# Score bounds in four column tiles and three rounds of 256 columns, and block 1's input added by VectorE in the tail

## The chip, the cores and the metric

The kernel runs on one core of a Trainium2 chip. A core has five engines with a queue each: TensorE (PE; its weight loads are listed as PEld), VectorE (DVE), ScalarE (ACT), GpSimd (POOL) and SyncE (SP), which here only issues DMAs. The metric is the time of one execution on the device in microseconds; smaller is better. Beside several timed executions there is one profiled execution, from which every duration in this document comes.

## The reference

The input `x` has 2048 rows of 640 values. It is normalized by row, goes through an attention with 32 heads of 20 values in four segments of 512 rows (softmax inside a segment, a linear memory over the segments before), and is multiplied by the gate of a gated feed-forward network:

```python
    x = A_x
    xn = _layernorm(x, axis=-1)
    s = _A_ref(xn, A_wq, A_wk, A_wv, A_wo, A_beta)
    g = _silu(_B_ref(xn, B_w_gate, B_w_up, B_w_down))
    return x + s * g
```

In `_A_ref`, for each segment:

```python
        logits = jnp.einsum('bhqd,bhkd->bhqk', qs, ks) * scale + mask
        p = _softmax(logits, axis=-1)
        a_dot = jnp.einsum('bhqk,bhkd->bhqd', p, vs)
        pq = phi(qs)
        num = jnp.einsum('bhld,bhde->bhle', pq, M)
        den = jnp.einsum('bhld,bhd->bhl', pq, z)[..., None] + 1e-06
        a_mem = num / den
        o = g * a_mem + (1.0 - g) * a_dot
```

## The kernel before

**Stages.** A segment is 512 rows (`L`), in four blocks `j` of 128. For each segment the kernel normalizes `x`, projects Q, K (`psq`) and V (`psv`), computes scores and exponentials, the products with V (`ApsT`), the memory part (`am`, `dm`), the gate and up products (`gp`, `up`, then `hT`), the down product (`yp`, then `aa`), and the output projection (`sp`). The product of `aa` and `sp` is added to `x` (the tile `xt`) and stored.

**Slots.** The scores are cut into units of four row tiles. A unit fills the PSUM tile `Sps` (one buffer of four banks), ScalarE takes its exponential into `pt`, GpSimd masks the diagonal. There are 81 units, and the loop over `slot` puts one of them after another on TensorE; in between, the rest of the work is issued by hand-set due times (`TIMES`) and by a rate. All instructions keep the order in which the program issues them on their engine. In a slot before a `visits` entry, `ORDER["columns"]` makes `mm` issue each matmul as four of 32 output columns, one for each column tile of the array (128*32 in the profile).

**Score bounds.** The exponential is taken without a row maximum; instead an upper bound of each score is subtracted inside the matmul. `q_abs` (L320) takes the absolute values of Q into `aq`, in two pieces of Q's five 128-row slices: slices 0 to 2 first, 3 and 4 later. `do_K` keeps the largest absolute value of each K row (`kabs`), and `bound` (L326) spreads them into a stationary operand `ik` of 32 columns, with a minus sign. `bound_mm` (L335) multiplies slice `c` of `ik` and `aq` into rows `32*(c%3)` and on of `cps`: three partial sums, in column tiles 0, 1 and 2, with 512 columns for each matmul. ScalarE casts `cps` to `cb` (L338), a DMA writes it to DRAM (`Bd`, L339), and `bound_dma` (L344, four DMAs for each half of the eight head groups) brings the partial rows behind the 20 rows of each head in `QT`. `KT` holds ones there, so `scores` (L546), with 23 rows, adds the three partial sums. The SP queue carries these DMAs between those of `relayout` (L313) for Q and K.

**PSUM.** Apart from `Sps`, all products take turns in four buffers (`ps_d`, tag `d`); a product waits until the buffer's last user has been read.

**Tail.** The last segment's `sp` are issued by hand at the end of the program. `tail_piece` (L532) multiplies half a block (128x320), VectorE multiplies it into `aa` (L535), then an engine adds `xt` (L538), and a queue stores (L541). Before the change GpSimd adds blocks 0 and 1 whole, when the second half is done, and block 2 in halves; VectorE adds block 3 in halves. Blocks 0, 1 and 3 are stored by SP, block 2 by ScalarE's queue. `tail_T4` transposes a piece for two blocks, with a copy by ScalarE (L524).

In the sections that follow, 1a and 1b are the halves of block 1, and so on; a "product" is L535, an "addition" L538.

Of the kernel before, what the change touches and what calls it, by code (L numbers as in the profile page):

```python
# [9 lines left out]
P = 128  # L10
D = 640
H = 32
DH = 20
E1 = DH + 1
NSEG = 4
L = 512
F = 1536
DC = D // P
# [63 lines left out]
def kernel(  # L82
# [14 lines left out]
    nc = tc.nc  # L97
    x2 = A_x.flatten_outer_dims()
    o2 = out.flatten_outer_dims()
# [11 lines left out]
    dpool = ctx.enter_context(tc.tile_pool(name="dscratch", bufs=1, space=bass.MemoryType.DRAM))  # L111
    Qd = [dpool.tile([D, L], BF, name=f"Qd{i}") for i in range(2)]
    Kd = [dpool.tile([D, L], BF, name=f"Kd{i}") for i in range(2)]
    Xd = [dpool.tile([L, D], BF, name=f"Xd{i}") for i in range(2)]
    Bd = [dpool.tile([3 * H, L], BF, name=f"Bd{i}") for i in range(2)]
    OTd = [dpool.tile([D, L], BF, name=f"OTd{i}") for i in range(2)]
    Od = [dpool.tile([L, D], BF, name=f"Od{i}") for i in range(2)]

# [5 lines left out]
    xt_of, xnT_of = {}, {}  # L124
# [24 lines left out]
    Wo = cpool.tile([P, DC, D], BF, name="Wo")  # L149
# [34 lines left out]
    KT = cpool.tile([P, NG, L], BF, name="KT")  # L184
    QT = cpool.tile([P, NG, L], BF, name="QT")
# [91 lines left out]
    seg = {}  # L277
# [51 lines left out]

    def bound_mm(n):  # L330
        ik, aq = seg[n]["bound"]
        cps = ps_d.tile([3 * H, L], F32, name="cps", tag="d")
        for c in range(DC):
            i = c % 3
            nc.tensor.matmul(cps[H * i:H * i + H, :], lhsT=ik[:, c, :], rhs=aq[:, c, :],  # L335
                             start=(c < 3), stop=(c >= 2), tile_position=(0, H * i), skip_group_check=True)
        cb = stg.tile([3 * H, L], BF, name="cb")
        nc.scalar.copy(cb[:], cps[:])  # L338
        nc.sync.dma_start(Bd[n % 2][:], cb[:])  # L339

    def bound_dma(n, half):
        src = Bd[n % 2][:].rearrange("(i r g) n -> r i g n", i=3, r=4)
        for r in range(4):
            nc.sync.dma_start(QT[32 * r + DH:32 * r + DH + 3, 4 * half:4 * half + 4, :],  # L344
                              src[r][:, 4 * half:4 * half + 4, :])

    def do_V(n, j, half, evac):
# [111 lines left out]
    def finish(steps):  # L459
        for _ in steps:  # L460
            pass
# [51 lines left out]
    def tail_T():  # L513
        nc.sync.dma_start_transpose(out=seg[NSEG - 1]["oTm"][:, 3, :], in_=Od[(NSEG - 1) % 2][:, C3:C4])

    def tail_add():
        oTm = seg[NSEG - 1]["oTm"][0:CUT, 3, :]
        nc.vector.tensor_tensor(oTm, oTm, seg[NSEG - 1]["oT"][0:CUT, 3, :], op=ALU.add)

# [3 lines left out]
            nc.tensor.transpose(po[:, j - j0, :], seg[NSEG - 1]["odot"][:, j, C4:D], ident[:])  # L523
        nc.scalar.copy(seg[NSEG - 1]["oT"][:, DC - 1, j0 * P:j1 * P].rearrange("p (j t) -> p j t", t=P), po[:])  # L524

    def tail_piece(j, h0, h1, add, store=None, queue=None):

        s, hs = seg[NSEG - 1], slice(h0, h1)
        sp = ps_d.tile([P, HD], F32, name="sp", tag="d")
        for c in range(DC):  # L530
            oT = s["oTm" if c == 3 else "oT"]
            nc.tensor.matmul(sp[:, 0:h1 - h0], lhsT=oT[:, c, j * P:(j + 1) * P], rhs=Wo[:, c, hs],  # L532
                             start=(c == 0), stop=(c == DC - 1), skip_group_check=True)
        aa, xr = s["aa"][j], xt_of[NSEG - 1][:, j, :]
        nc.vector.tensor_tensor(aa[:, hs], aa[:, hs], sp[:, 0:h1 - h0], op=ALU.mult)  # L535
        if add is not None:
            a0 = store[0] if store else h0
            add.tensor_tensor(xr[:, a0:h1], aa[:, a0:h1], xr[:, a0:h1], op=ALU.add)  # L538
        if store:
            t0 = (4 * (NSEG - 1) + j) * P  # L540
            queue.dma_start(o2[t0:t0 + P, store[0]:store[1]], xr[:, store[0]:store[1]])  # L541

    def scores(unit):
        for r in range(4):
            for (g, kb, c0, ncol, q0) in unit:
                nc.tensor.matmul(Sps[:, r, c0:c0 + ncol],  # L546
                                 lhsT=KT[32 * r:32 * r + DH + 3, g, kb * P:(kb + 1) * P],
                                 rhs=QT[32 * r:32 * r + DH + 3, g, q0:L],
                                 start=True, stop=True, tile_position=(32 * r, 0))

    def exps(unit):
# [208 lines left out]
    SLOTS, SEG = len(units), 20  # L760
# [27 lines left out]
    def old_attend(slot):  # L788
        attend(NSEG - 1, units[slot][1], pts[slot])
# [17 lines left out]
    for n in range(NSEG):  # L807
        t0 = n * SEG

        def on(name, ns, fn, *items):  # L810
            times = TIMES[name]
            for i, it in enumerate(items):
                at(t0 + (times[i] if isinstance(times, (list, tuple)) else times), ns, fn, *it)

        if n >= 1:
            on("dot6", 0, dot_spill, (n - 1, 4, 7))
            on("load6", 0, out_load, (n - 1, 0, C4))
            on("dot7", 0, dot_spill, (n - 1, 7, 8))
            on("load7", 0, out_load, (n - 1, C4, D))
            if n >= 2:  # L820
                on("add", 0, out_add, (n - 1, 0, DC - 1), (n - 1, DC - 1, DC))
            on("out", V_NS, out_item, *[(n - 1, i) for i in range(8)])
            on("update", 700, m_update, (n - 1,))
            on("mem", MEM_NS, mem_part, *[(n, i % 4, i // 4) for i in range(8)])
            on("mem_spill", 0, mem_spill, (n,))
            on("mem_T_last" if n == NSEG - 1 else "mem_T", 0, mem_T, (n,))
            if n < NSEG - 1:
                on("k_tok", 0, k_tok, (n,))
        on("dot3", 0, dot_spill, (n, 0, 4))
        if n == NSEG - 1:  # L830
# [12 lines left out]
        on("V", V_NS, do_V, *[(m, i // 2, i % 2, EVAC[TIMES["V_eng"][i]]) for i in range(8)])  # L843
        on("k_spill0", 0, spill, (m, 0, nc.sync, None))
        on("k_lay0", 0, relayout, (m, 0, Kd, KT, nc.sync))
        on("q_spill0", 0, spill, (m, 0, None, nc.sync))
        on("q_lay0", 0, relayout, (m, 0, Qd, QT, nc.sync))
        on("q_spill1", 0, spill, (m, 1, None, nc.sync))
        on("k_spill1", 0, spill, (m, 1, nc.sync, None))
        on("q_abs", 0, q_abs, (m, 0, 3), (m, 3, DC))  # L850
        on("bound", 0, bound, (m,))
        on("bound_mm", C_NS, bound_mm, (m,))
        on("bound_lay0", 0, bound_dma, (m, 0))
        at(t0 + SEG - 0.003, 0, relayout, m, 1, Kd, KT, nc.sync)
        at(t0 + SEG - 0.002, 0, relayout, m, 1, Qd, QT, nc.sync)
        at(t0 + SEG - 0.001, 0, bound_dma, m, 1)
        for name, sg, key in (("phi_k", n, "ktok"), ("phi_q", m, "qt")):
            for i, (c0, c1) in enumerate(((0, 2), (2, 4 if key == "ktok" else 5))):
                for fn, t, a in zip((phi_min, phi_exp, phi_end), TIMES[name][i], ((sg, key, c0, c1), (), ())):
                    at(t0 + t, 0, fn, *a)  # L860
        if n + 2 < NSEG:
            on("load_x", 0, load_x, (n + 2,))
    at(SLOTS - 2.001, 0, tail_spill)
    at(SLOTS - 1.001, 0, tail_T)
    at(SLOTS - 0.001, 0, tail_add)

    events.sort(key=lambda e: e[:2])
    events = deque(events)
# [32 lines left out]
    for slot, (n, unit) in enumerate(units):  # L901
        if slot in visits:
            m, g, us = visits[slot]
# [24 lines left out]
    finish(held[1][3])  # L928
    tail_T4(0, 2)
    old_attend(SLOTS - 1)  # L930
    tail_piece(0, 0, HD, None)
    tail_piece(0, HD, D, nc.gpsimd, (0, D), nc.sync)
    finish(held[0][3])
    tail_piece(1, 0, HD, None)
    tail_piece(1, HD, D, nc.gpsimd, (0, D), nc.sync)
    tail_T4(2, 4)
    tail_piece(2, 0, HD, nc.gpsimd, (0, HD), nc.scalar)
    tail_piece(2, HD, D, nc.gpsimd, (HD, D), nc.scalar)
    tail_piece(3, 0, HD, nc.vector, (0, HD), nc.sync)
    tail_piece(3, HD, D, nc.vector, (HD, D), nc.sync)  # L940

_INS = ['A_x', 'A_wq', 'A_wk', 'A_wv', 'A_wo', 'A_beta', 'B_x', 'B_w_gate', 'B_w_up', 'B_w_down']
_OUTS = [((1, 2048, 640), 'bfloat16')]
# [24 lines left out]
```

## Time and profile before

| | |
|---|---|
| median of three runs | 320.7 us (320.14, 320.99, 320.7) |
| the profiled execution's own time | 319.95 us |
| its span, first to last instruction | 318.2 us |
| granted TensorE clock, mean | 0.997 |
| PE, DVE, ACT, POOL busy | 312.3, 229.3, 227.2, 136.6 us |
| `cps` matmuls | 20, of 379 to 390 ns |
| `cb` casts | 4, of 581 to 612 ns |
| additions on POOL in the tail | 2 of 128x640 (1392 ns), 2 of 128x320 (789 ns) |
| additions on DVE in the tail | 2 of 128x320 (597 ns in the mean) |

How to read it: the span is the time between the first and the last instruction of the profiled execution; its own time has what lies around that too. A matmul's duration has the passage through the array in it, and matmuls overlap; how fast they follow each other is read from their starts. In a timeline each line has the start and the duration in us, the engine, the line of the code, the operation, out<-in, the shape and a count; in square brackets stands the engine's idle time before it and what ended it. A line with a count over 1 covers several instructions in a row. The chain of waits goes back from the last instruction: at each step to what released it, or to the instruction before it on its engine.

### The profile page before, as it was taken

How to read it: one execution, taken by the hardware profiler on the slowest of the kernel's cores; microseconds unless marked ns; L12 is line 12 of the kernel's file. 1: busy time of each engine (PE TensorE's matmuls, PEld its weight loads, DVE VectorE, ACT ScalarE, POOL GpSimd, SP SyncE). 2: the span in 40 equal slices, each digit the busy share in tenths (PEclk: the TensorE clock that was granted, in tenths of full speed). 3: DMA queues.
4: the chain of work that ended last, by engine and by line, in shares of the span. 5: the costliest groups of instructions: out<-in, count | busy, mean ns of one | idle time of the engine just before them, and what ended most of it. 6: DMA issues, size and time to landing. Idle time of an engine off the chain costs nothing.

```text
span 318.2 us, 10079 instructions
## 1 busy us (share of the span) xinstructions
PE 312.3 (98%) x4244; PEld 167.1 (53%) x4244; DVE 229.3 (72%) x503; ACT 227.2 (71%) x229; POOL 136.6 (43%) x231
## 2 busy tenths in 40 slices
PE   8999999999999999999999999999999999999994
PEld 3544445665555445654675455545466545445673
DVE  6474356756869888997679999977787687634555
ACT  3723477787898877777998768678897766776730
POOL 1870036435263445334453454445433353535324
PEclk9999999999999999999999999999999999999998
DMA  8984986410752362406583373235723000350302
GB/s 256 355 333 140 305 217 178 108 41 2 217 150 71 105 149 91 123 23 194 182 206 101 115 128 111 79 129 190 179 86 115 19 23 31 119 126 2 100 19 82
DMA packets 56086, 41.36 MB, mean 130 GB/s; under 512 B 26953, under 2 KB 54665, under 8 KB 56041
## 3 DMA queue, kind: packets, MB, share of 16 engines
q1 hardware_dynamic: 53496, 35.97, 39.9%
q10 hardware_dynamic: 2544, 4.75, 4.1%
q8 instruction: 33, 0.54, 0.7%
q14 instruction: 13, 0.10, 0.1%
HBM read 19.90 MB, written 14.78 MB: 109 GB/s over the span
## 4 chain that ended last, share of the span: by engine, by line
PE 97%; ACT 1%; DVE 1%; issue 0%; ACTq 0%
PE up L130 11%; PE yp L130 11%; PE gp L130 10%; PE psq L130 10%; PE Sps L546 9%; PE gp L134 6%; PE up L134 6%; PE yp L134 6%; PE psv L130 6%; PE ApsT L570 5%; PE psq L134 4%; PE sp L130 3%; PE sp L134 3%; PE sp L532 2%; PE psv L134 1%; PE wps L642 1%
## 5 line engine op out<-in xcount | busy, mean ns | idle before, releaser
L554 ACT ACTIVATE pt<-Sps 128x2048 bf16<-128x2048 f32 (+1 forms) x81 | 150.3, 1856 | 40.8 <-PE Sps L546 36.0
L556 POOL TENSOR_SCALAR_AFFINE_SELECT pt<-pt 128x512 bf16<-128x512 bf16 x128 | 83.0, 664 | 158.0 <-ACT pt L554 157.9
L438 DVE SCALAR_TENSOR_TENSOR hT<-tg,up 128x512 bf16<-128x512 bf16 x48 | 32.4, 674 | 23.3 <-PE up L130 8.7
L130 PE MATMUL up<-xnT,Wu 128*128 128x512 bf16 x160 | 43.0, 380 | 0.0
L130 PE MATMUL yp<-Wd,hT 128*128 128x320 bf16 x257 | 40.1, 300 | 0.0
L130 PE MATMUL gp<-xnT,Wg 128*128 128x512 bf16 x150 | 39.3, 380 | 0.0
L427 ACT ACTIVATE tg<-gp 128x512 bf16<-128x512 f32 x48 | 28.6, 596 | 14.3 <-PE gp L130 11.0
L546 PE MATMUL Sps<-QT,KT 23*128 23x128 bf16 (+3 forms) x512 | 32.6, 301 | 0.2
L589 DVE STREAM_TRANSPOSE obT<-ob 128x512 bf16<-128x512 bf16 x30 | 21.1, 704 | 13.3 <-POOL ob L585 13.3
L130 PEld LDWEIGHTS <-hT 128*128 128x128 bf16 x257 | 23.5, 98 | 11.6 <-issue 3.0
L455 DVE SCALAR_TENSOR_TENSOR aa<-t,yp 128x320 bf16<-128x320 bf16 x32 | 15.3, 478 | 14.5 <-ACT t L454 14.3
L134 PE MATMUL gp<-xnT,Wg 128*32 128x512 bf16 x360 | 24.1, 380 | 0.0
L591 DVE STREAM_TRANSPOSE tb<-ApsT 128x512 f32<-128x512 f32 x30 | 21.2, 708 | 2.4 <-PE ApsT L570 2.1
L130 PEld LDWEIGHTS <-Wu 128*128 128x128 bf16 x160 | 14.3, 98 | 16.2 <-issue 3.2
L546 PEld LDWEIGHTS <-KT 23*128 23x128 bf16 x512 | 10.0, 92 | 24.5 <-issue 24.4
L570 PE MATMUL ApsT<-pt,V 128*32 128x512 bf16 (+2 forms) x480 | 22.7, 299 | 0.0
L130 PEld LDWEIGHTS <-Wg 128*128 128x128 bf16 x150 | 14.1, 98 | 16.0 <-issue 1.9
L134 PE MATMUL up<-xnT,Wu 128*32 128x512 bf16 x320 | 21.7, 380 | 0.0
L454 ACT ACTIVATE t<-yp 128x320 bf16<-128x320 f32 x32 | 13.9, 435 | 10.4 <-PE yp L130 8.7
L130 PE MATMUL psv<-Wv,xnT 128*128 128x320 bf16 x130 | 20.8, 299 | 0.3
L585 POOL TENSOR_TENSOR ob<-tb,rb 128x320 bf16<-128x320 f32 x27 | 19.8, 732 | 2.2
L134 PE MATMUL yp<-Wd,hT 128*32 128x320 bf16 x508 | 20.0, 300 | 0.0
(122 smaller groups left out, 449.9 us busy)
## 6 DMA issues: line engine op xcount, KB each, us to landing
KT<-Kd SPq DMA_DIRECT2D x32, 80.0 KB
QT<-Qd SPq DMA_DIRECT2D x32, 80.0 KB
out_dram<-xt SPq DMA_DIRECT2D x14, 160.0 KB
Wg<-in_B_w_gate_dram ACTq DMA_DIRECT2D x1, 1920.0 KB
Wu<-in_B_w_up_dram ACTq DMA_DIRECT2D x1, 1920.0 KB
xt<-in_A_x_dram SPq DMA_DIRECT2D x3, 640.0 KB
Wd<-in_B_w_down_dram SPq DMA_DIRECT2D x1, 1920.0 KB
Xd<-xn SPq DMA_DIRECT2D x12, 160.0 KB
```

The lines of the kernel that those rows point to most:

```text
L130: nc.tensor.matmul(out_, lhsT=lhsT, rhs=rhs, start=start, stop=stop, skip_group_check=True)
L134: nc.tensor.matmul(out_[cols], lhsT=lhsT[:, cols], rhs=rhs, start=start, stop=stop, tile_position=(0, 32 * r), skip_group_check=True)
L427: nc.scalar.activation(tg[:], gp[:], ACT.Tanh, scale=0.5)
L438: nc.vector.scalar_tensor_tensor(out=h[:], in0=seg[n]["tg"][:], scalar=1.0, in1=up[:], op0=ALU.add, op1=ALU.mult)
L455: nc.vector.scalar_tensor_tensor(out=s["aa"][j][:, hs], in0=t2[:], scalar=1.0, in1=yp[:], op0=ALU.add, op1=ALU.mult)
L546: nc.tensor.matmul(Sps[:, r, c0:c0 + ncol], lhsT=KT[32 * r:32 * r + DH + 3, g, kb * P:(kb + 1) * P], rhs=QT[32 * r:32 * r + DH + 3, g, q0: ...
L554: nc.scalar.activation(pt[:, :, 0:ntot], Sps[:, :, 0:ntot], ACT.Exp, scale=SCALE)
L556: nc.gpsimd.affine_select(out=pt[:, :, c0:c0 + P], in_=pt[:, :, c0:c0 + P], compare_op=ALU.is_ge, fill=0.0, base=0, pattern=[[0, 4], [1, P ...
L570: nc.tensor.matmul(ps[32 * r:32 * r + 32, q0:L], lhsT=Vflat[n % 2][:, off:off + 32], rhs=t[:, r, c0:c0 + ncol], start=(i == 0), stop=(i == ...
L585: nc.gpsimd.tensor_tensor(ob[:, :, 0:DH], tb[:, :, 0:DH], rb[:].unsqueeze(2).to_broadcast([P, L // 32, DH]), op=ALU.mult)
L589: nc.vector.transpose(s["obT", g // 4][:, g % 4, :], ob[:].rearrange("p b e -> p (b e)"))
L591: s["turn", g] = (lambda: nc.vector.transpose(tb[:].rearrange("p b e -> p (b e)"), ps[:]), quotients, turn_back)
```

## The change

`bound_mm` now makes four partial sums in four column tiles. Ten matmuls of 256 columns take the place of five of 512: slices 0 to 3 in column tiles 0 to 3, first for the left half of the columns, then for the right half; then slice 4 for the left half in column tile 0 and for the right half in column tile 1. `Bd`, `cb` and the rows in `QT` grow from three partial rows to four, and `scores` multiplies 24 rows. In segments 1 to 3 `q_abs` takes slices 0 to 3 first and slice 4 later; in segment 0 its pieces stay.

In the tail, block 1's `x` is added by VectorE in two halves, and no longer by GpSimd whole: 1a is added after product 1b, and 1b after product 2a. SP stores block 1 after that, whole as before. The additions of the other blocks stay with their engines.

```diff
-    Bd = [dpool.tile([3 * H, L], BF, name=f"Bd{i}") for i in range(2)]
+    Bd = [dpool.tile([4 * H, L], BF, name=f"Bd{i}") for i in range(2)]
...
     def bound_mm(n):
         ik, aq = seg[n]["bound"]
-        cps = ps_d.tile([3 * H, L], F32, name="cps", tag="d")
-        for c in range(DC):
-            i = c % 3
-            nc.tensor.matmul(cps[H * i:H * i + H, :], lhsT=ik[:, c, :], rhs=aq[:, c, :],
-                             start=(c < 3), stop=(c >= 2), tile_position=(0, H * i), skip_group_check=True)
-        cb = stg.tile([3 * H, L], BF, name="cb")
+
+        cps = ps_d.tile([4 * H, L], F32, name="cps", tag="d")
+        jobs = [(i, i, h) for h in range(2) for i in range(4)] + [(4, h, h) for h in range(2)]
+        for c, i, h in jobs:
+            hs = slice(h * L // 2, (h + 1) * L // 2)
+            nc.tensor.matmul(cps[H * i:H * i + H, hs], lhsT=ik[:, c, :], rhs=aq[:, c, hs],
+                             start=(c < 4), stop=(c == 4 or i != h), tile_position=(0, H * i),
+                             skip_group_check=True)
+        cb = stg.tile([4 * H, L], BF, name="cb")
         nc.scalar.copy(cb[:], cps[:])
         nc.sync.dma_start(Bd[n % 2][:], cb[:])
 
     def bound_dma(n, half):
-        src = Bd[n % 2][:].rearrange("(i r g) n -> r i g n", i=3, r=4)
+        src = Bd[n % 2][:].rearrange("(i r g) n -> r i g n", i=4, r=4)
         for r in range(4):
-            nc.sync.dma_start(QT[32 * r + DH:32 * r + DH + 3, 4 * half:4 * half + 4, :],
+            nc.sync.dma_start(QT[32 * r + DH:32 * r + DH + 4, 4 * half:4 * half + 4, :],
                               src[r][:, 4 * half:4 * half + 4, :])
...
-    def tail_piece(j, h0, h1, add, store=None, queue=None):
+    def tail_piece(j, half):
...
-        aa, xr = s["aa"][j], xt_of[NSEG - 1][:, j, :]
-        nc.vector.tensor_tensor(aa[:, hs], aa[:, hs], sp[:, 0:h1 - h0], op=ALU.mult)
-        if add is not None:
-            a0 = store[0] if store else h0
-            add.tensor_tensor(xr[:, a0:h1], aa[:, a0:h1], xr[:, a0:h1], op=ALU.add)
-        if store:
+        nc.vector.tensor_tensor(s["aa"][j][:, hs], s["aa"][j][:, hs], sp[:], op=ALU.mult)
+
+    def tail_add(j, h0, h1, eng, queue=None):
+
+        hs = slice(h0 * HD, h1 * HD)
+        xr = xt_of[NSEG - 1][:, j, hs]
+        eng.tensor_tensor(xr, seg[NSEG - 1]["aa"][j][:, hs], xr, op=ALU.add)
+        if queue is not None:
             t0 = (4 * (NSEG - 1) + j) * P
-            queue.dma_start(o2[t0:t0 + P, store[0]:store[1]], xr[:, store[0]:store[1]])
+            queue.dma_start(o2[t0:t0 + P, hs], xr)
 
     def scores(unit):
...
-                                 lhsT=KT[32 * r:32 * r + DH + 3, g, kb * P:(kb + 1) * P],
-                                 rhs=QT[32 * r:32 * r + DH + 3, g, q0:L],
+                                 lhsT=KT[32 * r:32 * r + DH + 4, g, kb * P:(kb + 1) * P],
+                                 rhs=QT[32 * r:32 * r + DH + 4, g, q0:L],
...
-        on("q_abs", 0, q_abs, (m, 0, 3), (m, 3, DC))
+        on("q_abs", 0, q_abs, (m, 0, 4), (m, 4, DC))
...
-    tail_piece(0, 0, HD, None)
-    tail_piece(0, HD, D, nc.gpsimd, (0, D), nc.sync)
+    tail_piece(0, 0)
+    tail_piece(0, 1)
+    tail_add(0, 0, 2, nc.gpsimd, nc.sync)
     finish(held[0][3])
-    tail_piece(1, 0, HD, None)
-    tail_piece(1, HD, D, nc.gpsimd, (0, D), nc.sync)
+    tail_piece(1, 0)
+    tail_piece(1, 1)
+    tail_add(1, 0, 1, nc.vector)
     tail_T4(2, 4)
-    tail_piece(2, 0, HD, nc.gpsimd, (0, HD), nc.scalar)
-    tail_piece(2, HD, D, nc.gpsimd, (HD, D), nc.scalar)
-    tail_piece(3, 0, HD, nc.vector, (0, HD), nc.sync)
-    tail_piece(3, HD, D, nc.vector, (HD, D), nc.sync)
+    tail_piece(2, 0)
+    tail_add(2, 0, 1, nc.gpsimd, nc.scalar)
+    tail_add(1, 1, 2, nc.vector)
+    t0 = (4 * (NSEG - 1) + 1) * P
+    nc.sync.dma_start(o2[t0:t0 + P, :], xt_of[NSEG - 1][:, 1, :])
+    tail_piece(2, 1)
+    tail_add(2, 1, 2, nc.gpsimd, nc.scalar)
+    tail_piece(3, 0)
+    tail_add(3, 0, 1, nc.vector, nc.sync)
+    tail_piece(3, 1)
+    tail_add(3, 1, 2, nc.vector, nc.sync)
```

The order of the instructions on every engine is otherwise the same as before; the old `tail_add`, which adds `oT` into `oTm` (L518), is now called `tail_sum`.

More of the change, by code (lines that the diff above doesn't have):

```diff
@@ L514, in tail_T, with tail_sum @@
         nc.sync.dma_start_transpose(out=seg[NSEG - 1]["oTm"][:, 3, :], in_=Od[(NSEG - 1) % 2][:, C3:C4])
-    def tail_add():
+    def tail_sum():
         oTm = seg[NSEG - 1]["oTm"][0:CUT, 3, :]
@@ L524, in tail_T4 @@
         nc.scalar.copy(seg[NSEG - 1]["oT"][:, DC - 1, j0 * P:j1 * P].rearrange("p (j t) -> p j t", t=P), po[:])
-    def tail_piece(j, h0, h1, add, store=None, queue=None):
-        s, hs = seg[NSEG - 1], slice(h0, h1)
+    def tail_piece(j, half):
+        s, hs = seg[NSEG - 1], slice(half * HD, (half + 1) * HD)
         sp = ps_d.tile([P, HD], F32, name="sp", tag="d")
@@ L531, in tail_piece @@
             oT = s["oTm" if c == 3 else "oT"]
-            nc.tensor.matmul(sp[:, 0:h1 - h0], lhsT=oT[:, c, j * P:(j + 1) * P], rhs=Wo[:, c, hs],
+            nc.tensor.matmul(sp[:], lhsT=oT[:, c, j * P:(j + 1) * P], rhs=Wo[:, c, hs],
                              start=(c == 0), stop=(c == DC - 1), skip_group_check=True)
-        aa, xr = s["aa"][j], xt_of[NSEG - 1][:, j, :]
-        nc.vector.tensor_tensor(aa[:, hs], aa[:, hs], sp[:, 0:h1 - h0], op=ALU.mult)
-        if add is not None:
-            a0 = store[0] if store else h0
-            add.tensor_tensor(xr[:, a0:h1], aa[:, a0:h1], xr[:, a0:h1], op=ALU.add)
-        if store:
+        nc.vector.tensor_tensor(s["aa"][j][:, hs], s["aa"][j][:, hs], sp[:], op=ALU.mult)
[4 more added lines that the diff above has]
+        if queue is not None:
             t0 = (4 * (NSEG - 1) + j) * P
-            queue.dma_start(o2[t0:t0 + P, store[0]:store[1]], xr[:, store[0]:store[1]])
+            queue.dma_start(o2[t0:t0 + P, hs], xr)
     def scores(unit):
@@ L864 @@
     at(SLOTS - 1.001, 0, tail_T)
-    at(SLOTS - 0.001, 0, tail_add)
+    at(SLOTS - 0.001, 0, tail_sum)
     events.sort(key=lambda e: e[:2])
```

## The prediction, made before the changed kernel was run

> **What bounds the kernel now.** I read the page first: engine shares, slices, and the chain of work that ended last.
>
> ```profile
> span 318.2 us, 10079 instructions
> ...
> PE 312.3 (98%) x4244; PEld 167.1 (53%) x4244; DVE 229.3 (72%) x503; ACT 227.2 (71%) x229; POOL 136.6 (43%) x231
> ...
> PE   8999999999999999999999999999999999999994
> ...
> PE 97%; ACT 1%; DVE 1%; issue 0%; ACTq 0%
> ```
>
> TensorE is busy in every slice but the first and the last, and 97% of the last chain is TensorE's. So a cut counts if it shortens TensorE's stream in the body, or what follows TensorE in the tail. Next I read the chain of the last 10 us (start, us, what):
>
> ```profile
> 311.28 2.15 PE sp L532 x15
> ...
> 313.45 0.50 DVE aa L535
> ...
> 313.97 0.87 DVE xt L538
> 314.84 0.41 DVE aa L535
> ...
> 315.27 0.32 DVE xt L538
> ```
>
> From 313.45 on VectorE sets the end: product and addition of block 3's first half, then of its second. Two equal additions (128x320) take 0.87 and 0.32 us. The timeline of GpSimd and VectorE says why the first is long (start, us):
>
> ```profile
> 309.22 1.39 POOL L538 TENSOR_TENSOR xt<-aa,xt 128x640 bf16<-128x640 bf16 x1 [5.57 <-DVE aa L535]
> 311.77 2.89 POOL L538 TENSOR_TENSOR xt<-aa,xt 128x640 bf16<-128x640 bf16 x3 [1.16 <-DVE aa L535]
> ...
> 264.56 0.49 DVE L502 TENSOR_TENSOR xt<-aa,xt 128x640 bf16<-128x640 bf16 x1
> ...
> 264.61 0.94 POOL L556 TENSOR_SCALAR_AFFINE_SELECT pt<-pt 128x512 bf16<-128x512 bf16 x1 [2.03 <-ACT pt L554]
> ```
>
> GpSimd's three additions (block 1 whole, block 2 in halves: 1.39, then 0.79 each by the groups) end at 311.77 + 2.89 = 314.66; VectorE's addition, begun at 313.97, ends at 314.84, 0.18 later. So the two shut each other out: VectorE's addition of two SBUF tiles ran when GpSimd was done. The rows at 264.6 show the other order: VectorE began 0.05 us earlier and kept its 0.49, and the select took 0.94 instead of its usual 0.63. Who begins first goes first; the other is late by what is left.
>
> Last, TensorE's timeline at the bounds of segment 1, and a `mem_part` in column tiles:
>
> ```profile
> 88.28 0.60 PE L134 MATMUL up<-xnT,Wu 128*32 128x512 bf16 x8
> 88.71 0.39 PE L335 MATMUL cps<-aq,ik 128*32 128x512 bf16 x3
> 88.72 0.38 PE L570 MATMUL ApsT<-pt,V 128*32 128x512 bf16 x1
> 88.93 0.38 PE L335 MATMUL cps<-aq,ik 128*32 128x512 bf16 x2
> 88.94 0.92 PE L570 MATMUL ApsT<-pt,V 128*32 128x512 bf16 x15
> 89.79 0.35 PE L546 MATMUL Sps<-QT,KT 23*128 23x384 bf16 x4
> ...
> 113.02 0.35 PE L134 MATMUL am<-Mbd,qtd 128*32 128x147 bf16 x12
> 113.20 0.39 PE L134 MATMUL up<-xnT,Wu 128*32 128x512 bf16 x4
> ```
>
> Three `cps` start together at 88.71 and two at 88.93: two rounds. `ApsT` of free column tiles slips in beside them, so each column tile has a stream of its own, and the tiles with two `cps` of 512 columns reach the next scores last.
>
> **The change part by part.** *Bounds on TensorE.* Five 512-column rows of the chain take 1.08 us, 0.216 a round; sixty `yp` of 320 columns in column tiles take 2.04, 0.136 a round. That is 0.417 ns a column and 3 ns a round, so a 256-column round takes 0.109. Two rounds of 512 are 0.432, three of 256 are 0.328: 0.104 less, four times (26.4, 88.7, 155.3, 221.7): **-0.41**. Bounds: nothing gained if ScalarE decides right behind (the exponential before the scores at 216.80 and 150.94 holds TensorE some 0.1 there), and a loss of 0.76 if all weight loads are exposed (below). I take -0.41: at all four places the chain runs through TensorE's rows.
>
> The Trainium skill, "TensorE: Matmul & The Clock Gate", Part 3, says that a weight load overlaps running matmuls only if its row group differs; all column tiles share their row groups. By that rule every round would also last as long as its load, and the sum would be the +0.42 of rival 3 in place of -0.75. The trace disagrees: above, twelve matmuls of 147, 147 and 84 columns, three rounds, pass in 0.18 us while each load (PEld) takes 0.10.
>
> *Around the bounds, at nothing.* The scores multiply 24 rows for 23: 23 rows with 512 columns take 0.38 as 128 rows do. The `cb` cast goes from 96 to 128 partitions: 0.59, and 128-partition casts of the same length (L288) take 0.585. `Bd` grows to 128 KB (4 issues), `QT<-Bd` to 16 KB (32 issues): 256 KB on 41.36 MB. An SP issue of 12 KB takes 0.23 to 0.30 and of 80 KB 0.28 to 0.55, so at most 0.05 more each; the tightest segment has its last issue of the first half at 165.50 and its first scores at 169.30: 3.8 us of cover, without which 0.2 would be lost. The absolute values take 0.55 for 1536 columns and 0.42 for 1024, 0.25 ns each, hence 0.68 and 0.29 in segments 1 to 3. The first now also waits for ScalarE's copy of the fourth slice, done 0.96 us before in segment 1 and more in the others. Behind it on VectorE the eviction of the fifth Q slice, an addition and a K eviction come 0.13 later, and TensorE needs their PSUM buffer: in segment 3 that eviction ends at 216.50 and the fourth tile after it starts at 218.23. Covered by 1.7 us; uncovered, 0.13 three times. The shorter second one is done earlier.
>
> *The tail.* TensorE's rows stay; from the old times: products 1a, 1b end at 311.70. Addition 1a (0.32) fills VectorE's 0.40 of idling before product 2a at 312.09, GpSimd being idle. Product 2a ends at 312.58. Then addition 1b (VectorE, at 312.60) and 2a (GpSimd, 0.07 after its releaser as at 311.77, so 312.65) meet; VectorE is first, as at 264.56, and 2a is late by 0.13: it ends at 312.65 + 0.79 + 0.13 = 313.57. Product 2b moves from 312.77 to 312.94 and ends at 313.43; product 3a keeps 313.45. Addition 2b on GpSimd: 313.53 to 314.32 (before 314.66). Addition 3a on VectorE waits for it and ends 0.18 later, 314.50 instead of 314.84; product 3b's TensorE work is done at 314.1. All behind moves by **-0.34**; block 1's store leaves SP at 313.0 instead of 313.2, in front of 3a's, which isn't ready before 314.5. Bounds: -0.55 if addition 3a runs at its free 0.32, +0.30 if GpSimd gets in first at 312.6 (addition 1b then ends at 313.62, product 2b at 314.1, GpSimd's last at 314.96, 3a at 315.14). I take -0.34, since VectorE needs no releaser there.
>
> Sum: -0.41 - 0.34 = **-0.75**. The profiled execution took 319.95 (span 318.2 and 1.7 around it) and would take 319.20. The median of the runs shown, 320.7, lies 0.75 above it; the same difference there gives **319.9**.
>
> **The rivals.** (1) *GpSimd first in the tail*, +0.30 instead of -0.34: total -0.11, 320.6. For it: only 0.05 us between the two starts; against it: 264.56, where 0.05 was enough. (2) *ScalarE keeps the pace*: scores wait for the exponential of the slot before, so what TensorE gains at `cps` is idled away before the next scores; total -0.34, 320.4. For it: the stalls near 150.94 and 216.80 (0.1 each); against it: the chain passes ScalarE for 1% only, and those exponentials hang on TensorE rows a few us earlier, which move too. (3) *Weights exposed, the slower side*: each `cps` round waits for its load of 0.097, three rounds last 0.62, not 0.33, +0.19 four times = +0.76, with the tail +0.42: 321.1. It decides as soon as a round takes over 0.144 (a third of 0.432). Against it stand the `am` rounds. This is what the rule cited above (the Trainium skill, "TensorE: Matmul & The Clock Gate", Part 3) would do here. (4) *The tail's clash vanishes*: -0.41 - 0.55 = -0.96, 319.7, if GpSimd's last ends before 313.97; it would have to start 0.35 earlier than product 2b allows. That the change doesn't do what it says is hardly open: the instruction order has ten `cps` of 256 columns and both additions on VectorE.
>
> **How the numbers follow.** Forecast 0.58, rivals 0.13, 0.14, 0.08, 0.07. A measurement of this kernel can tell about 0.3%, 0.96 us, from no change; the three runs shown lie 0.85 apart, so half of that is added around every case. The forecast's -0.75 lies just inside the band: I give a third of it to faster (0.20), with rival 4 and a little of 2 (0.06 and 0.03) 0.29, rounded to 0.3. Slower by over 0.96 needs rival 3 together with rival 1 or an unforeseen wait: 0.07. The range takes rival 4 less 0.6 of spread at the bottom and rival 3 at the top: 319.1 to 321.1.
>
> **What would show it.** Right: `cps` as ten matmuls of 256 columns in three rounds 0.11 apart, the next scores 0.1 nearer; GpSimd's last addition ends some 0.35 nearer to TensorE's last `sp`, addition 3a near 0.5 instead of 0.87; product 2b begins 0.17 later; span near 317.5. Wrong: rounds of 0.15 or more; GpSimd's addition 2a at 0.79 while VectorE's 1b takes about 1.0; TensorE idling longer before scores; a product 3a that starts after its matmuls are long done.

## The result, and the profile after

| | before | after |
|---|---|---|
| median of the runs made together, us | 320.48 (11 runs) | 321.65 (11 runs) |
| ratio after : before | | 1.0043, 95% interval 1.0027 to 1.0059 |
| profiled execution's own time, us | 319.95 | 321.65 |
| its span, us | 318.2 | 319.9 |

The kernel became slower by 0.43%; the forecast was slightly faster. 321.65 us lies above the range as well. The two medians differ by 1.17 us and the two profiled executions by 1.70, since that of before lies 0.53 below its median. The page of the kernel after:

```profile
span 319.9 us, 10120 instructions
...
PE   8999999999999999999979999999999999999995
...
q8 instruction: 33, 0.54, 0.7%
...
PE 96%; issue 1%; ACT 1%; DVE 1%; ACTq 0%
```

TensorE's row has a 7 in the 21st slice, where there was a 9, and 1% of the chain is now "issue". So one place lost time. The gains first. TensorE's timeline at the bounds of segment 1, kernel after:

```profile
88.67 0.50 PE L337 MATMUL cps<-aq,ik 128*32 128x256 bf16 x10
88.90 0.81 PE L575 MATMUL ApsT<-pt,V 128*32 128x512 bf16 x16
89.64 0.41 PE L551 MATMUL Sps<-QT,KT 24*128 24x384 bf16 x8
```

From the first `cps` to the next scores it is 89.64 - 88.67 = 0.97 us; before, it was 89.79 - 88.71 = 1.08. The single matmuls start in three rounds, 0.11 apart. Then the tail, in the chain of waits of the kernel after (start, us, what):

```profile
315.58 0.50 DVE aa L537
316.08 0.02 issue
316.10 0.42 DVE xt L543
316.53 0.41 DVE aa L537
316.94 0.02 issue
316.96 0.33 DVE xt L543
```

Addition 3a takes 0.42 in place of 0.87. What the gains and the loss amount to is read by laying the starts of the 81 score units of the two traces beside each other; where the difference changes, something was gained or lost:

| place | change, us |
|---|---|
| bounds of segments 0, 1, 2, 3 | -0.04, -0.10, -0.10, -0.10 |
| between the starts of units 38 and 39 (162 to 169 us) | +2.54 |
| unit 39 to 40 (0.23 that before lost there), unit 40 to 41 | -0.23, +0.23 |
| unit 70 to 71 (0.06 that before lost there) | -0.06 |
| tail | -0.44 |
| sum (rounded from three places) | +1.70 |

The gains that were forecast came, bounds and tail together -0.8 for -0.75, and one stall of 2.5 us buried them. It lies at the end of segment 1, after the third of the four bounds (the expectations below say "end of segment 2" for it, as its bounds are those of segment 2). The chain of waits there, kernel after:

```profile
163.73 0.64 PE dm L394 x80
164.37 1.36 PE yp L134 x40
165.74 0.54 PE ApsT L575 x15
166.27 2.28 issue
168.55 0.27 PE ApsT L575
```

Fifteen of sixteen `ApsT` run, then TensorE does nothing for 2.28 us, and no semaphore is named for it ("issue"). The sixteenth reads the same tiles as the fifteenth. The same view of the kernel before has a small one of this kind a little further on:

```profile
167.65 0.14 PE psv L130
167.78 0.07 issue
167.85 1.38 PE psv L130 x9
```

In what follows, a stall is how much later a matmul starts than the columns of the one ahead of it need: 2.45 us in after, 0.23 in before ("issue" is some 0.16 less, as it counts from a modelled end).

What TensorE can run out of without a semaphore is instructions. The page counts 33 packets in queue q8 with 0.54 MB in sum, 16 KB each, and TensorE has 4264 matmuls and as many weight loads: 258 for each packet (257 in before). The DMA view of two windows of the kernel after, 157.1 to 165.9 and 165.9 to 167.2 us (packets, MB, share):

```profile
q1 hardware_dynamic: 3597, 1.68, 81.7%
q14 instruction: 1, 0.01, 0.2%
...
q8 instruction: 1, 0.02, 5.6%
```

The same of the kernel before, 165.2 to 166.5 us:

```profile
q1 hardware_dynamic: 205, 0.22, 48.7%
q8 instruction: 1, 0.02, 6.0%
```

In after no q8 packet runs for 8.8 us; then one does, from 166.00 to 167.16, and TensorE goes on 1.39 us after its end. In before it ran from 165.24 to 166.49, and TensorE went on 1.36 us after. So the theory, T1 in the expectations: TensorE's instructions come in packets of 256, and this one was late. The burst of `dm`, 80 short matmuls with 80 loads in 0.64 us, uses them up fast; each new bound adds five matmuls and five loads, so at the third bound 30 instructions more have gone by, and the edge between two packets falls 30 instructions earlier in the work. In the two traces no packet sets out more than 290 instructions ahead of the one at which TensorE would have to stop without it. Here these 290 started within 3.67 us in before and within 2.85 in after; ahead of no other edge of the two kernels within less than 3.47. Other packets, too, set out only up to 4.3 us after that point (this one 1.4 in before and 2.9 in after), and cost nothing, since TensorE took longer over their instructions. The rivals: the larger loads of the bounds crowd the DMA queues (T2), or chance (T3).

### The profile page after: what moved, and what is told of

Its sections match the earlier page's. It is cut to its first block, busy times and chain, and to the rows that moved or that the text cites. A ratio compares the mean times of both kernels' runs of the same rounds, so it can differ in the third digit from the quotient of the medians.

```text
span 319.9 us, 10120 instructions
## 1 busy us (share of the span) xinstructions
PE 312.4 (98%) x4264; PEld 168.1 (53%) x4264; DVE 229.8 (72%) x505; ACT 226.9 (71%) x229; POOL 134.7 (42%) x230
## 4 chain that ended last, share of the span: by engine, by line
PE 96%; issue 1%; ACT 1%; DVE 1%; ACTq 0%
PE up L130 11%; PE yp L130 11%; PE gp L130 10%; PE psq L130 10%; PE Sps L551 9%; PE gp L134 6%; PE up L134 6%; PE yp L134 6%; PE psv L130 6%; PE ApsT L575 5%; PE psq L134 4%; PE sp L130 3%; PE sp L134 3%; PE sp L535 2%; PE wps L647 1%; PE psv L134 1%
## 5 line engine op out<-in xcount | busy, mean ns | idle before, releaser
L551 PE MATMUL Sps<-QT,KT 24*128 24x128 bf16 (+3 forms) x512 | 32.7, 300 | 0.1
L551 PEld LDWEIGHTS <-KT 24*128 24x128 bf16 x512 | 10.0, 92 | 27.1 <-issue 26.7
```

Of the source, the lines that this page charges most:

```text
L551: nc.tensor.matmul(Sps[:, r, c0:c0 + ncol], lhsT=KT[32 * r:32 * r + DH + 4, g, kb * P:(kb + 1) * P], rhs=QT[32 * r:32 * r + DH + 4, g, q0: ...
```

## The experiments

Medians are of runs made together with the kernel before, whose median stands beside them; the ratio is to the latter.

### The two halves of the change

Tail alone: the kernel before with `tail_piece`, `tail_add` and the calls of the change. Bounds alone: the rest.

> The new tail alone, the old bounds. Theory T1 (TensorE starved of instructions: the ten TensorE instructions that each new bound adds bring the stream earlier to the edge of a 256-instruction packet, in the burst after segment 2, and the packet is late): no TensorE instruction is added before the tail, so no stall of 2.5 us near 166 us, and the time is the kernel before's less the tail's gain, about -0.45 us (-0.3 to -0.6). Theory T2 (the new bounds' loads, four partial rows instead of three, crowd the DMA queues there): the same here. If the stall came from the tail's code or from chance (T3), it shows here too: +1.5 us or more.

> The new bounds alone, the old tail. T1 and T2 both: the stall of after at the end of segment 2, some 2.3 to 2.6 us of TensorE waiting for nothing that the profile shows, less 0.23 us of it that the kernel before has as well and less 0.31 us that three bounds save: +1.5 to +2.2 us over the kernel before. T3 (chance): the stall anywhere or not at all, -0.3 us if not.

| | median, before | ratio, interval | stall |
|---|---|---|---|
| tail alone | 320.04, 320.68 | 0.9984, 0.9964 to 1.0004 | 0.38, at the second `psv` as in before |
| bounds alone | 322.31, 320.68 | 1.0057, 1.0034 to 1.0080 | 2.12, at the sixteenth `ApsT` as in after |

The loss belongs to the bounds. In the profile the tail alone is worth -0.45, as in after. The profiled execution of bounds alone was the longest of its runs, 323.73 us, and it shows what a stall can bring with it: from 170 to 172 us, right behind it, the granted clock was 0.50, and ten `psv` took 2.67 us in place of 1.36. A mean clock of 0.995 or less was granted in 3 of the 11 runs of after and in 4 of the 11 of bounds alone, but only in 2 of the 152 runs of before that the tables of this section compare with.

### More instructions, the same work

30 more (the same columns of warm-up in more matmuls), and 14 more with `range(16)` and 288 columns:

```diff
-    keep_warm(9)
+    for _ in range(24):
+        nc.tensor.matmul(wps[:, 0:192], lhsT=warm[:, 0:P], rhs=warm[:, 0:192], start=True, stop=True)
```

> The kernel before, with 30 more TensorE instructions in the warm-up ahead of everything (nine matmuls of 512 columns become 24 of 192, the same columns in sum) and nothing else. T1: the edge of the late packet moves to where after has it, and a stall of 1.5 to 2.6 us appears at the end of segment 2 though no work and no transfer of the kernel has changed: +1.3 to +2.3 us over the kernel before. T2 and T3: as the kernel before, within 0.3 us, stall there no longer than its 0.23 us.

> The kernel before with 14 more TensorE instructions in the warm-up (16 matmuls of 288 columns in place of nine of 512, the same columns). T1: between the kernel before and the one with 30 more; by the starts of the instructions in the trace of before the packet has 1.0 us less time, nearly what 30 cost it: a stall of 1.0 to 2.2 us, +0.7 to +2.0 us. If the loss were in proportion to the instructions added: a stall of about 1.2 us.

286 more, which is 30 and a packet:

```diff
-    keep_warm(9)
+    for _ in range(38):
+        for r in range(4):
+            nc.tensor.matmul(wps[32 * r:32 * r + 32, 0:120], lhsT=warm[:, 32 * r:32 * r + 32],
+                             rhs=warm[:, 0:120], start=True, stop=True, tile_position=(0, 32 * r),
+                             skip_group_check=True)
```

> The kernel before with 286 more TensorE instructions in the warm-up (38 rounds of four column tiles of 120 columns): 30 and one whole packet of 256. T1: the edges fall as with 30 more, and the stall of 2.0 to 2.5 us is back at the same place: +1.3 to +2.3 us. If the number of instructions ahead matters and not the edge, or if the form of the warm-up does: no such stall, or one elsewhere.

| | median, before | ratio, interval | stall |
|---|---|---|---|
| before + 14 | 321.62, 320.51 | 1.0041, 1.0023 to 1.0059 | 2.00 |
| before + 30 | 322.82, 320.68 | 1.0068, 1.0044 to 1.0091 | 2.26 |
| before + 286 | 323.49, 320.60 | 1.0088, 1.0057 to 1.0119 | 2.21 |

The old bounds and the old tail, with nothing but a warm-up cut finer some 160 us earlier, have the stall. The chain of waits of before + 30:

```profile
166.03 0.53 PE ApsT L570 x15
166.56 2.10 issue
168.66 0.27 PE ApsT L570
```

of before + 286, a whole packet on:

```profile
166.01 0.54 PE ApsT L570 x15
166.54 2.05 issue
168.59 0.27 PE ApsT L570
```

and of before + 14:

```profile
166.88 0.33 PE Sps L546 x7
167.21 1.84 issue
169.05 0.21 PE Sps L546
```

The place moves by the instruction. The work goes on as `ApsT`, eight `Sps`, five `yp`, `psv`, each matmul with its load. In before the second `psv` is late. Thirty instructions, 15 matmuls, ahead of it is the sixteenth `ApsT`: that one is late with 30 and with 286. Seven ahead is the eighth `Sps`: that one is late with 14. T2 and T3 can't do this. (The profiled execution of before + 14 was the longest of its runs, 323.76 us, and here too the clock was 0.50 from 170 to 172 us, behind the stall.) Before + 286 has the stall that was expected, but its time, 2.9 us above that of before, lies over the 1.3 to 2.3 expected; 3 of its 7 runs have a mean clock of 0.995 or less, and the rest is not explained.

### Fewer instructions for the new bounds

Six matmuls a bound, the same columns on the longest tile:

```diff
-        jobs = [(i, i, h) for h in range(2) for i in range(4)] + [(4, h, h) for h in range(2)]
-        for c, i, h in jobs:
-            hs = slice(h * L // 2, (h + 1) * L // 2)
+        jobs = [(i, i, 0, L) for i in range(4)] + [(4, h, h * L // 2, (h + 1) * L // 2) for h in range(2)]
+        for c, i, h0, h1 in jobs:
+            hs = slice(h0, h1)
...
-                             start=(c < 4), stop=(c == 4 or i != h), tile_position=(0, H * i),
+                             start=(c < 4), stop=(c == 4 or i > 1), tile_position=(0, H * i),
```

> The changed kernel with six matmuls for each bound in place of ten: the four first chunks at 512 columns, the fifth in two halves of 256 on two column tiles. Columns on the longest tile, partial rows, loads and tail are those of the changed kernel; at the third boundary 6 TensorE instructions more than in the kernel before have gone by in place of 30. T1: by the starts of the instructions in the trace of before, 6 instructions leave the late packet 0.6 us less time and 30 leave it 1.1 us less, and it was also longer on its way with 30: a stall of 0.5 to 1.5 us in place of 2.5, and a time from 0.6 us below to 0.4 us above the kernel before. A theory by which the four partial rows and their loads make the packet late: the stall of 2.1 to 2.5 us stays, +1 to +1.6 us over the kernel before.

320.11 us beside 320.51 (0.9989, 0.9976 to 1.0002), 1.5 us less than after. The chain of waits:

```profile
166.89 0.51 PE yp L130 x3
167.40 0.34 issue
167.75 0.43 PE yp L130 x2
```

Six instructions are three matmuls, and three ahead of the second `psv` is the fourth `yp`: there TensorE stops, for 0.51. The three later bounds gain 0.11 each, as with ten matmuls, and the tail its 0.44. Partial rows, loads and tail are those of after, so T2 is out.

### What makes the packet late

The transposing DMA `oTm<-Od` runs on SP just there. First it is replaced by a plain copy, in before + 30; this leaves out the transposing for segment 1, whose output is then in the wrong order:

```diff
-        nc.sync.dma_start_transpose(out=seg[n]["oTm"][:], in_=Od[n % 2][:])
+        if n == 1:
+            nc.sync.dma_start(seg[n]["oTm"][:].rearrange("p c n -> p (c n)").rearrange("p (j d) -> p j d", j=4),
+                              Od[n % 2][:].rearrange("(j p) d -> p j d", p=P))
+        else:
+            nc.sync.dma_start_transpose(out=seg[n]["oTm"][:], in_=Od[n % 2][:])
```

> The kernel before with 30 more TensorE instructions in the warm-up, and the transposing DMA of the memory's output that runs at the end of segment 2 (161 to 165 us) replaced by a plain copy of as many bytes; the output of segment 1 is therefore left permuted. If the packet is late because the burst uses up instructions faster than any packet can come: the stall of 2.1 to 2.3 us stays. If it is late because the burst falls where the transposing DMA keeps the DMA engines full (share of 16 engines above 1.0 from 163 to 166 us): the packet starts within 0.5 to 1.4 us of its request, as others do, and the stall falls to 0 to 0.9 us, 1.3 to 2.3 us below the kernel with 30 more alone.

Then the transposing DMA is kept and issued earlier, `mem_T=12.0` for `mem_T=16.8` in `TIMES`, in after and with six matmuls:

> The changed kernel with one thing moved: the transposing DMA of the memory's output (oTm<-Od) is issued at slot 12.0 of a segment in place of 16.8, right behind the spill that it reads, so that it runs near 146 us and not at 161 to 165 us. TensorE's instructions and their order are those of the changed kernel. T1 with the DMA load as its second half (the packet is late since the burst asks for it while SP's transposing DMA and the loads behind it fill the DMA engines): taking the transposing out of that place shortened the stall from 2.3 to 1.4 us with 30 instructions more in the kernel before, so here from 2.5 to 1.2 to 1.9 us: 0.6 to 1.3 us below the changed kernel, 0 to +0.6 us over the kernel before. If only the count of instructions matters: the stall of 2.3 to 2.6 us stays, +1.0 to +1.3 us over the kernel before.

> The changed kernel with six matmuls a bound and the transposing DMA early: no padding. T1 with the DMA load: the stall of 0.5 us that six matmuls left falls to 0 to 0.3 us, and the time to 0.7 to 1.1 us below the kernel before. If the count alone matters: as with six matmuls alone, 0.4 us below.

| | median, before | ratio, interval | stall (without the edit) |
|---|---|---|---|
| before + 30, plain copy | 321.71, 320.51 | 1.0055, 1.0032 to 1.0077 | 1.43 (2.26) |
| after, early | 321.83, 320.27 | 1.0053, 1.0036 to 1.0071 | 1.39 (2.45) |
| six matmuls, early | 321.38, 320.27 | 1.0034, 1.0007 to 1.0060 | 0.33 (0.51) |

Neither theory of the plain copy has its numbers: 0.8 us of the stall went there, and 1.1 with the early transposing in after; 1.4 stayed in both. By these two profiles the load on the DMA engines is a part of the lateness. But with less of it (shares of 0.57, 0.84 and 0.75 in the three us from 163 on in after with the early transposing; 0.85, 1.08 and 1.36 in after) the burst still outruns the packet. The early transposing helped nobody: the loads of the next segment stand behind it on SP. In after, `Kd<-ktd` left SP by 150.1 us and `KT<-Kd` at 156.6; with the early transposing they left by 155.8 and at 161.9, SP's timeline (start, us):

```profile
148.83 2.85 SPq L471 DMA_TRANSPOSE oTm<-Od  x1
...
154.76 1.08 SPq L307 DMA_DIRECT2D Kd<-ktd  x1
161.86 1.48 SPq L313 DMA_DIRECT2D KT<-Kd  x4
```

The store `Qd<-qtd` also came 5.3 us later than in after, and VectorE waited for it:

```profile
168.45 0.56 DVE L370 TENSOR_SCALAR qtd<-qtd 128x1536 bf16<-128x1536 bf16 x1 [4.26 <-DMA Qd<-qtd]
```

Behind that, `psv` waited 1.3 us at 171.4, which it does not in after. The times expected of both early ones did not come; the stall expected of after did, and that of six matmuls nearly (0.33, where 0 to 0.3 was expected).

### Moving the edge away

126 more instructions: the 286 of above with `range(18)` and 256 columns. 110 more: whole-array matmuls as in the 30, with `range(64)` and 72 columns.

> The changed kernel with 126 more TensorE instructions in the warm-up (nine matmuls of 512 columns become 18 rounds of four column tiles of 256 columns). T1: the edge falls far from the burst of segment 2, the stall is gone, and the time is that of the gains alone: 0.75 to 1.0 us below the kernel before (about 319.6), unless another packet becomes late. T2 and T3: the stall stays, about +1.2 us over the kernel before as the changed kernel.

> The kernel before, with the same 126 more TensorE instructions in the warm-up as the run before gave the changed kernel. T1: what the kernel before itself loses at the end of segment 2 (0.23 us in its profile, 0.38 us in the profile with the new tail alone) goes: 0.2 to 0.6 us below the kernel before, and the realigned changed kernel stays 0.75 to 1.0 us below this one, which is then the worth of the change without the late packet. If padding is worth nothing where the stall is small, or the gain of the realigned changed kernel came from its warm-up: as the kernel before within 0.2 us, or as far below it as the other, 1.6 us.

> The changed kernel with 110 more TensorE instructions in the warm-up, in another form than the 126: 64 matmuls of 72 columns on the whole array in place of nine of 512 (the same columns). T1: the edge of the packet lies 16 instructions from where 126 put it, still far from the burst: no stall, 0.8 to 1.6 us below the kernel before, as with 126. If the four column tiles of the other warm-up gave the gain: +0.8 to +1.3 us over the kernel before, as the changed kernel.

> The kernel before with the same 110 more. T1: its own small stall goes; where the bounds' loads into QT take over, as they did with 126 more, nothing is gained: from 0.4 us below the kernel before to 0.2 above. If the padding itself harms (as in half of the runs with 126): +0.6 to +1.0 us.

> The changed kernel with six matmuls a bound and 110 more TensorE instructions in the warm-up. T1: no stall at the end of segment 2; the time of the padded changed kernel, within 0.3 us, since the bounds take as long with six matmuls as with ten. If ten shorter matmuls are themselves a gain over six: slower than the padded changed kernel by the 0.3 us that three bounds gained.

> The changed kernel with 126 more TensorE instructions in the warm-up, the kernel that took 319.04 us, once more. If that time belongs to it: 1.3 to 1.8 us below the kernel before again. If the loads into QT behind the transposing DMA are late in some runs and not in others, whatever the warm-up: 0 to 1.2 us below, with runs near 318.9 us and runs a microsecond longer.

> Six matmuls a bound with the same warm-up of 126 more. If the warm-up on four column tiles makes the time: as the one with ten matmuls a bound in the same call, within 0.4 us. If the edge does: the edge lies 24 instructions from that of the other at the end of segment 2 and 8 from that of the one with six matmuls and 110 more, whose time (320.4 us) it then has within 0.4 us.

And both kernels with 126 more and the transposing early:

> The kernel before with 126 more TensorE instructions in the warm-up and the transposing DMA early. The run without the early transposing was slower than the kernel before though its late packet was gone. If the loads of the bounds into QT, which stand behind the transposing DMA on SP, took over as the last wait there (the four Sps at 169 us started 0.125 us apart, as their four loads landed; the transposing took 3.1 to 5.1 us in different profiles): they land some 3 us earlier now, the four Sps start together, and the time is 0.2 to 0.6 us below the kernel before, with no run near 321.5 us but for the odd one. If the loss came from the warm-up or from elsewhere: 321 us as without the early transposing.

> The changed kernel with 126 more TensorE instructions in the warm-up and the transposing DMA early. In the profile of the padded changed kernel the loads of the bounds into QT landed late and cost 0.87 us at 169 us, though most of its timed runs were 0.8 us shorter than the profiled one. If the transposing ahead of them caused that: no such wait, a profiled span of 317.0 to 317.4 us, and 1.3 to 1.8 us below the kernel before with less spread. If the transposing is only moved into another wait (the loads of the next segment's input stand behind it at 146 us): slower than without the move.

No stall for instructions is left at the end of segment 1 in any of the nine. What the first scores of segment 2 (unit 40, near 169 us) waited in the profile stands last.

| | median (lowest), before | ratio, interval | `Sps` waits |
|---|---|---|---|
| after + 126 | 319.04 (318.86), 320.68 | 0.9952, 0.9933 to 0.9972 | 0.41 |
| the same again | 319.17 (318.95), 320.64 | 0.9964, 0.9952 to 0.9976 | 0.94 |
| six + 126 | 320.15 (318.89), 320.64 | 0.9987, 0.9958 to 1.0016 | 2.77 |
| after + 110 | 320.89 (319.40), 320.60 | 1.0019, 0.9989 to 1.0049 | 1.25 |
| six + 110 | 320.39 (319.46), 320.60 | 0.9996, 0.9979 to 1.0014 | under 0.2 |
| before + 126 | 321.31 (320.18), 320.51 | 1.0025, 1.0005 to 1.0044 | under 0.2 |
| before + 110 | 320.63 (319.92), 320.60 | 1.0001, 0.9984 to 1.0018 | under 0.2 |
| before + 126, early | 320.96 (320.07), 320.27 | 1.0013, 0.9994 to 1.0032 | 0.33 |
| after + 126, early | 320.29 (318.81), 320.27 | 0.9985, 0.9968 to 1.0002 | under 0.2 |

The changed kernel with its edge moved is the fastest version found, by its medians 1.6 and 1.5 us below the kernel before on two occasions, more than the 0.75 to 1.0 expected at first. Its lowest runs lie only 1.0 and 0.9 below the lowest of before (319.88 and 319.89); what more the medians show is that fewer of its runs are long, and why is not shown. The profile with the early transposing, 318.81 us, shows the change with hardly a wait in the way: a span of 317.1, 1.15 less than before. That is 0.31 for the three later bounds, 0.45 for the tail, 0.23 for the old stall and the 0.06 at unit 71, less 0.12 lost at unit 41; another 0.23 lie ahead of the first unit, where the other profiles scatter too.

But an edge moved away is not all. Behind the late packet stands a second wait with nearly the same due time. The chain of waits of six + 126:

```profile
164.87 0.41 DVE dmb L399
...
166.19 4.77 DMA Kd<-ktd
...
171.04 0.47 DMA KT<-Kd
171.51 0.01 issue
171.52 0.96 PE Sps L551 x4
```

The first scores of segment 2 wait for the segment's loads. In after + 126 the view names `QT<-Bd`, in before + 126 with the early transposing `QT<-Qd`; in two others it names ScalarE's `t`, which the scores don't read, so there the cause is not shown. Even the kernel before has hardly any slack here: with 126 more, unit 40 began 0.23 earlier against the units ahead of it, and unit 41 had lost those 0.23 again, since the four `Sps` then start 0.125 apart. In the profile that is why padding the kernel before gained nothing. Seven of its twelve runs with 126 took over 321.1 us, which no profile caught and nothing here explains. The times expected of before + 126, of after + 110, of six + 110 and of the early transposing did not come: they reckoned with the packet alone. Nor is it the warm-up on four column tiles that makes after + 126 fast, since six + 126 has the same one and the time of six + 110. Why after + 126 is fast in most runs and its neighbours are not stays open.

## Why the prediction was wrong

*The bounds on TensorE, -0.41: right in kind, a little large.* The rounds are 0.11 apart, as worked out, and segments 1 to 3 gained 0.10 each. Segment 0's rounds gained as much (from the first `cps` to the next `gp` 26.39 to 26.93, then 26.47 to 26.91), but started 0.08 later, so that 0.02 was left, and 0.04 from unit 7 on. Measured: -0.35. The weight loads stayed hidden, and rival 3 is out. The rule of the Trainium skill, "TensorE: Matmul & The Clock Gate", Part 3, would have had each round last longer by its load; the trace of after does not agree, with its rounds of 0.11.

*The tail, -0.34: mis-sized, -0.45 measured* (the same within 0.01 in the tail alone and with six matmuls). GpSimd's and VectorE's timelines of the kernel after:

```profile
314.79 1.55 POOL L543 TENSOR_TENSOR xt<-aa,xt 128x320 bf16<-128x320 bf16 x2 [2.04 <-DVE aa L537]
...
314.23 0.49 DVE L537 TENSOR_TENSOR aa<-aa,sp 128x320 bf16<-128x320 bf16 x1 [0.16 <-PE sp L535]
314.63 0.32 DVE L543 TENSOR_TENSOR xt<-aa,xt 128x320 bf16<-128x320 bf16 x1
314.90 0.49 DVE L537 TENSOR_TENSOR aa<-aa,sp 128x320 bf16<-128x320 bf16 x1
```

VectorE was first, as chosen. But addition 1b does not need product 2a, and it began at 314.63, 0.09 before that product's end (314.23 + 0.49); the prediction had put it 0.02 behind the end, as for an addition that reads its product. So only 0.16 of addition 1b was left when GpSimd began 2a at 314.79, and 2a took 0.81, late by 0.02 and not by 0.13. Product 2b was not pushed back by 0.17 either: it began 2.13 after its old time, as the whole tail did. So GpSimd's last addition ended 0.45 earlier against TensorE (316.35) and not 0.34, and addition 3a ended 0.18 behind it, as worked out. That the two gains together came so near to -0.75 is luck: the one was too large by 0.06, the other too small by 0.11.

*Around the bounds, at nothing: here it failed.* That part priced casts, issues, rows and absolute values, and left out that ten matmuls are ten instructions and ten loads, where five and five had been. These instructions were put at nothing without a reason, and the runs showed +2.54 us in their place. Nothing of it shows at the bounds; it shows 11 us further, where a burst meets the edge of a packet. The profile had the warning: the `dm` burst and an "issue" of 0.07 in the chain at 167.78, beside a `psv` that no one held up. The prediction did not look for it, since the share of "issue" on the page was 0%. No rival had this mechanism, and rivals 1 and 2 did not occur either; an "unforeseen wait" stands in the prediction only as a part of the chance of 0.07 for slower.

The page of the Trainium skill "Runtime: NRT & Kernel Launch", section "Instruction fetch mechanics", says that each engine's instructions come in blocks of 16 KB, 256 of them, over a DMA queue that the sequencer drives itself, and that crossing a block is mostly hidden. The packets of q8 agree on the size. In the traces of before and after 32 of the 33 cost nothing; the one in the burst cost 0.2 us before and 2.5 after.

What is settled: the loss is a late packet of TensorE's instructions, set by how many instructions went before. In the seven profiles that hold every matmul and have the stall (before, after, before + 14, the plain copy, six matmuls, and the two early ones without padding), TensorE stops at the same count: 4289 of its instructions in the trace come ahead, though the matmul is a `psv`, an `ApsT`, an `Sps` or a `yp`. Open is why the packet also set out later with the edge earlier (166.0 in place of 165.2); less load on the DMA engines there took 0.8 to 1.1 us off the stall.

## What to carry to other kernels

Splitting matmuls has a price that no row of the split work shows: more instructions. Where a kernel has bursts of short matmuls, look in the chain for "issue" on TensorE, count the instructions ahead of it, and try the change with the edge moved: a few matmuls cut finer in the warm-up tell, by where the stall then stands in the trace, whether a loss belongs to the work or to the edge. The time alone may not tell: of the kernels with the edge moved away only one has an interval wholly below 1. Prefer the form with the fewest instructions (six matmuls here, not ten): an edge that padding has moved away moves again with every later edit that adds or takes away instructions.

## What the runs showed of the hardware

- TensorE went on 1.23 to 1.47 us after the end of the late q8 packet in the profiles with a stall of over 0.5 us. In the traces of before and after no packet sets out more than 290 instructions ahead of the one at which TensorE would stop without it: it holds little more than one packet of 256 ahead.
- How many instructions went by 160 us earlier moved the time by 0.4% to 0.9%, with the work unchanged (14, 30 and 286 more in the warm-up).
- Behind a stall of some 2 us TensorE's clock is halved in some runs: in the profiles of bounds alone and of before + 14 the granted clock was 0.50 from 170 to 172 us, and ten `psv` took 2.67 and 2.43 us in place of 1.36. In the profiles of after and of before + 30, with stalls of 2.45 and 2.26, it stayed at 1.00.
- Two GpSimd operations that began while VectorE was adding two SBUF tiles were late by less than VectorE had left: 0.31 late with 0.44 left (the select at 264.61 in before), 0.02 late with 0.16 left (2a at 314.79 in after: 0.81 us, the next one 0.79).
